# Attention tiles of two heads of both batches, a full-width g, and an h contracted over 64 rows with the batches side by side

## The chip, the cores and the metric

The kernel runs on one core of one Trainium2 chip. Times are device microseconds (us) of one launch on that core. The time before is the median of three runs, 1415.34 us (1413.17 to 1415.9). The profile comes from one more execution of its own, which took 1413.25 us; its span from the first to the last instruction is 1411.5 us.

## The reference, cut to what matters

Three layers follow each other. The first is a linear attention with 32 memory slots per head (8 batches, 8 heads, 576 positions, 64 columns a head), the second a maximum over three products, the third a gated one.

```python
a    = softmax(phi over the sequence)                 # 576 x 32 a head
k_m  = a.T @ k ;  v_m = a.T @ v                       # 32 x 64 a head
attn = softmax(q @ k_m.T / 8)                         # 576 x 32 a head
x    = attn @ v_m                                     # heads side by side: 4608 x 512
h    = max(x @ w1, x @ w2, x @ w3)                    # 4608 x 768
x2   = h @ w_out                                      # 4608 x 512
out  = (sigmoid(x2 @ w_gate) * (x2 @ w_val)) @ w_out2 # 4608 x 512
```

The kernel never forms x. For each batch it multiplies v_m by w1, w2 and w3 first, which gives g (256 rows for the 8 heads and their 32 slots), and then h = max over the three of g.T @ attn. The weights arrive as 64-bit floats and are turned into 32-bit ones on the chip. Products that need more than one pass split each operand into a high and a low part and add three passes (low by high, high by low, high by high).

## The kernel before, in words

**Phases.** The batches are taken in four pairs, p = 0 to 3. A pair has an *h stage* of 24 steps and an *x2 stage* of 16 steps; after the last pair comes the third layer (`up`, `down`), which the change does not touch. A prelude ahead of pair 0 loads and computes the first four attention tiles.

**Attention tiles.** Tile n = 4p .. 4p+3 is one batch and four of its heads, 128 partitions of 4 heads by 32 slots. Six stages make it: `a0` (exponential of phi), `a1` (transposes), `a2` (a.T @ [k v], four 32-column products side by side on TensorE, then a copy of each head's 32 rows into a zeroed block-diagonal tile), `a3` (transposes; `vt` is filled from two batches), `a4` (scores, two 64-column products side by side), `a5` (softmax), and `a_split` (high and low part, the tile `attn`). The tiles of pair p+1 are made between the steps of pair p.

**The h stage.** For every block j of 128 columns of h (6 blocks) there are four steps u, one for each batch and half of the sequence. `g_step` (line 342) makes 128 rows of g for block j+1 with three matmuls of 384 columns: 64 rows belong to one batch, 64 to the other, and they go to two different tiles, so that each of g's tiles holds 128 rows (4 heads) of one batch. They are copied out as two pieces of 64 partitions on ACT (line 356), and the low part is made by two subtractions on DVE (line 73; on POOL for 6 of the steps of pair 0). `h_step` (line 369) then runs 18 matmuls of 128 contracted rows by 288 columns into three PSUM banks, ACT copies one bank (line 379), DVE takes two maxima (lines 380, 381), ACT or DVE writes the high part (lines 68, 70) and POOL the low part.

**The x2 stage.** `x2_step` (line 392): 18 matmuls of 128 rows by 288 columns over all six blocks of h, one copy (three buffers), one store.

**Weights.** Each of 80 pieces of weights is loaded as 64-bit words into a ring of three buffers (`raw`), turned into floats by two ACT operations (lines 122, 123) and three DVE operations (lines 124, 125, 126, the last of which frees the buffer), and then split into high and low parts (w1 to w3, w_out) or stored again as floats (`wbf`, the 48 pieces of the third layer, `b_step`). In the program 24 pieces of w1 to w3 and 8 of w_out belong to the prelude and to pair 0; the 48 pieces of the third layer are asked for from pair 1 on. Pairs 1 to 3 load the split w1 to w3 back (`wxs`).

**What sets the order.** All transfers are issued from the SP queue, in order. On each engine the instructions stand in one fixed order, which a list scheduler chooses when the program is built, from its own model of how long each instruction takes: an instruction whose inputs are ready early in that model can be put ahead of instructions that the program writes before it. On the chip each engine then works through its list strictly in that order and waits where an input is not there. The eight PSUM banks are one pool (`bank()`).

Of the kernel before, what the change touches and what calls it, by code (L numbers as in the profile page):

```python
# [18 lines left out]
def attn_moe_kernel(  # L19
# [15 lines left out]
    J = wx.shape[0]  # L35
# [101 lines left out]
    def early(shape):  # L137

        t = low.tile([128, 2 * U], F32R, tag="h", name="early", bufs=4 * J)
        return f32(t[:, :shape[1]])  # L140

    def load_phi(n):
        st = A[n] = {"kv": [], "q": []}
        if n in (2, 3):
            st["phi"] = early([128, S])
        else:
            st["phi"] = att.tile([128, S], F32, tag="phi", name="phi", bufs=2)
        dma(st["phi"], phiT[n])

    def load_kv(n):  # L150
        for c in range(5):
            if n < 4:
                t = early([128, 512])
            else:
                t = att.tile([128, 512], F32, tag="kv", name="kv", bufs=7)
            if c < 4:
                dma(t, kvm[n, c])
            else:
                dma(t[:64], kvt[n])
            A[n]["kv"].append(t)  # L160

    def load_q(n, e):
        if (n, e) in ((0, 0), (0, 1)):
            t = early([128, S])
        else:
            t = att.tile([128, S], F32, tag="q", name="q", bufs=3)
        dma(t, qT[n, e])
# [3 lines left out]
    KVB = []  # L171
    for i in range(2):
        t = att.tile([128, 2, 2, 64], F32, name=f"kvb{i}")
        pool.memset(t, 0.0)
        KVB.append(t)

    def a0(n):
# [8 lines left out]
        vec.reciprocal(out=rs, in_=rs)  # L186
        yield
# [12 lines left out]
    def a2(n):  # L200
# [13 lines left out]
        kvb = st["kvb"] = KVB[n % 2]  # L214
        for s in range(4):
            r = slice(32 * s, 32 * s + 32)
            act.activation(out=kvb[r, :, s % 2], in_=p[r, :128].rearrange("p (x d) -> p x d", x=2),
                           func=AF.Copy, scale=st["rs"][r])
# [3 lines left out]
    def a3(n):  # L222
        st = A[n]
        b, g = divmod(n, 2)
# [6 lines left out]
        if b % 2 == 0:  # L231
            VT[b // 2, g] = mid.tile([128, 2, 4, 64], F32R, tag="vt", name="vt", bufs=4)
        vt = VT[b // 2, g]
        src = p[:, 128:256].rearrange("p (h m) -> p h m", h=2)
        for h in range(2):
            x = 3 * h if b % 2 == 0 else 2 - h
            act.copy(vt[:, 0, x], src[:, h])
            sub(vec, vt[:, 1, x], src[:, h], f32(vt[:, 0, x]))
# [95 lines left out]
    def g_step(p, j, hp):  # L334
        g, e = divmod(hp, 2)
        if e == 0:
            for b in range(2):
                G[b, j, g] = mid.tile([128, 2, 384], F32R, tag=f"g{b}", name=f"g{b}", bufs=3 + b)
# [530 lines left out]
```

## Time and profile before

| what | value |
| --- | --- |
| median of three runs | 1415.34 us |
| the profiled execution, its time / its span | 1413.25 / 1411.5 us |
| TensorE (PE) busy, share of the span | 1353.1 us, 96% |
| DVE / ACT / POOL busy | 875.0 / 583.3 / 517.7 us |
| prelude, until the first h matmul | 0 to 51 us |
| pair 0: h stage, x2 stage | 51 to 160, 160 to 212 us |
| pair 1: h stage, x2 stage | 212 to 298, 298 to 350 us |
| pair 2: h stage, x2 stage | 350 to 429, 429 to 473 us |
| pair 3: h stage, x2 stage | 473 to 540, 540 to 578 us |
| third layer | 578 to 1411 us |

The stage limits are the starts and ends of the matmuls of lines 369 and 392 in the trace. All four pairs do the same h and x2 work; pairs 0 to 2 also make attention tiles, and the weight pieces fall into the first two. A row of the stage view gives the time of the stage, then for each engine its busy time and its instructions, then the granted clock of TensorE, the busy share of the DMA engines and what they moved. A group row ends with busy time and mean time of one, and then the idle time ahead of the group and who ended it.

### The profile page before, as it was taken

Reading aid. Unit: us, or ns where it says so; the run is one execution under the profiler, and the core shown is the slowest. Engines: PE = TensorE matmul, PEld = TensorE weight load, DVE = VectorE, ACT = ScalarE, POOL = GpSimd, SP = SyncE. Lnnn points to the kernel's source line nnn. Section 1 sums busy time; section 2 is a strip of 40 time slices with the busy share of each in tenths; the row PEclk is TensorE's granted clock in tenths of the full one; section 3 lists DMA queues with packets and bytes.
Section 4 is the critical chain, followed back from the end, with each engine's and each line's share of the span. In section 5 each row is a group of like instructions: output and inputs, shape, how many; then the busy total and the mean of one; then the engine's idle time right before and its main releaser. Section 6 shows DMA issues by size and latency. Waiting matters only on the chain.

```text
span 1411.5 us, 22167 instructions
## 1 busy us (share of the span) xinstructions
PE 1353.1 (96%) x7864; PEld 1191.1 (84%) x7864; DVE 875.0 (62%) x1532; ACT 583.3 (41%) x1236; POOL 517.7 (37%) x456
## 2 busy tenths in 40 slices
PE   6588899989999999999999999999999999999998
PEld 3478798879999999878888888888888899999997
DVE  5989989987773575667765344454454534554454
ACT  6768667754653353353333221232222322133221
POOL 2666422241233126554487111371112712161211
PEclk8779999999999999999999999999999999999999
DMA  9588799878552433775546554465454666566651
GB/s 316 192 260 278 257 328 321 291 249 276 185 162 92 159 95 119 281 265 213 204 175 228 167 179 161 160 198 194 149 168 175 209 219 229 188 230 225 223 202 67
DMA packets 112269, 292.43 MB, mean 207 GB/s; under 512 B 12576, under 2 KB 28960, under 8 KB 112160
## 3 DMA queue, kind: packets, MB, share of 16 engines
q1 hardware_dynamic: 112160, 291.03, 60.8%
q8 instruction: 62, 1.02, 0.3%
q14 instruction: 47, 0.39, 0.1%
HBM read 224.92 MB, written 66.06 MB: 206 GB/s over the span
## 4 chain that ended last, share of the span: by engine, by line
PE 80%; DVE 7%; DMA 5%; issue 3%; ACT 3%; POOL 1%; SPq 0%; DVEq 0%; POOLq 0%; ACTq 0%
PE po L754 21%; PE px L687 15%; PE ps L369 11%; PE pz L687 10%; PE pv L687 10%; PE ps L392 8%; PE ps L342 3%; DMA raw<-wb_dram 1%; DVE ca L124 1%; DVE g L73 1%; PE ps L245 1%; DVE ca L126 1%; ACT g L356 1%; PE ps L207 1%; DMA q<-qT_dram 1%
## 5 line engine op out<-in xcount | busy, mean ns | idle before, releaser
L754 PE MATMUL po<-wo,gg 128*128 128x512 f32 x1296 | 332.8, 395 | 1.0 <-POOL gg L73 1.0
L73 POOL TENSOR_TENSOR gg<-gf,gg 128x512 fp32r<-128x512 f32 (+1 forms) x120 | 143.5, 1196 | 478.1 <-ACT gg L720 478.1
L754 PEld LDWEIGHTS po<-wo,gg 128*128 128x128 f32 x1296 | 242.5, 188 | 55.2 <-POOL gg L73 1.5
L369 PE MATMUL ps<-attn,g 128*128 128x288 f32 x1728 | 258.3, 304 | 18.3 <-POOL s L73 5.6
L369 PEld LDWEIGHTS ps<-attn,g 128*128 128x128 f32 x1728 | 247.5, 195 | 26.1 <-POOL s L73 5.9
L687 PE MATMUL px<-xa,tb 128*128 128x512 f32 (+1 forms) x1080 | 245.3, 369 | 1.6 <-ACT sg L710 1.3
L766 DVE TENSOR_TENSOR acc<-po,acc 128x512 f32<-128x512 f32 x180 | 124.3, 691 | 182.7 <-PE po L754 182.2
L687 PEld LDWEIGHTS px<-xa,tb 128*128 128x128 f32 x1080 | 198.1, 188 | 31.6 <-POOL tb L73 1.7
L687 PE MATMUL pz<-xa,tb 128*128 128x512 f32 (+1 forms) x720 | 171.0, 370 | 0.4 <-DVE x L70 0.4
L687 PE MATMUL pv<-xa,tb 128*128 128x512 f32 (+1 forms) x720 | 170.6, 369 | 0.0
L392 PE MATMUL ps<-h,wo 128*128 128x288 f32 x1152 | 161.4, 299 | 0.0
L392 PEld LDWEIGHTS ps<-h,wo 128*128 128x128 f32 x1152 | 157.3, 192 | 2.2 <-issue 1.9
L73 POOL TENSOR_TENSOR h<-hm,h 128x288 fp32r<-128x288 f32 x96 | 82.9, 865 | 196.7 <-ACT h L68 102.8
L687 PEld LDWEIGHTS pz<-xa,tb 128*128 128x128 f32 x720 | 132.2, 188 | 20.7 <-DVE x L70 0.8
L687 PEld LDWEIGHTS pv<-xa,tb 128*128 128x128 f32 x720 | 131.8, 188 | 18.9
L720 ACT CAST gg<-gf 128x512 fp32r<-128x512 f32 (+1 forms) x120 | 69.4, 579 | 179.6 <-DVE gf L716 132.7
L738 DVE TENSOR_TENSOR u<-pz,p 128x512 f32<-128x512 f32 (+1 forms) x120 | 76.2, 635 | 95.3 <-PE pz L687 89.2
L73 DVE TENSOR_TENSOR g<-ps,g 64x384 fp32r<-64x384 f32 x180 | 99.3, 552 | 32.7 <-ACT g L356 29.3
L356 ACT CAST g<-ps 64x384 fp32r<-64x384 f32 x192 | 90.7, 474 | 56.4 <-PE ps L342 30.4
L710 ACT ACTIVATE sg<-sg 128x512 f32<-128x512 f32 (+1 forms) x90 | 53.1, 590 | 146.8 <-DVE sg L708 146.6
L73 POOL TENSOR_TENSOR xa<-xf,xa 128x512 fp32r<-128x512 f32 (+1 forms) x64 | 78.7, 1252 | 19.9 <-ACT xa L131 19.9
L342 PE MATMUL ps<-wx,vt 128*128 128x384 f32 x288 | 73.0, 365 | 7.3 <-DVE g L73 3.0
(91 smaller groups left out, 1415.6 us busy)
## 6 DMA issues: line engine op xcount, KB each, us to landing
tb<-tbs SPq DMA_DIRECT2D x168, 512.0 KB, 3.7
wx<-wxs SPq DMA_DIRECT2D x72, 384.0 KB, 4.1
wo<-wos SPq DMA_DIRECT2D x48, 512.0 KB, 5.1
tbs<-tb SPq DMA_DIRECT2D x42, 512.0 KB, 2.9
raw<-wb_dram SPq DMA_DIRECT2D x48, 384.0 KB, 4.8
kv<-kvm_dram SPq DMA_DIRECT2D x48, 256.0 KB, 5.2
raw<-wx_dram SPq DMA_DIRECT2D x24, 384.0 KB, 4.0
wxs<-wx SPq DMA_DIRECT2D x24, 384.0 KB, 5.0
```

What stands on the lines that cost most here:

```text
L73: eng.tensor_tensor(out=o, in0=a, in1=b, op=ALU.subtract)
L124: vec.tensor_scalar(out=ai, in0=ai, scalar1=3, scalar2=None, op0=ALU.logical_shift_left)
L342: pe.matmul(ps[:, :384], lhsT=vt[:, x, 2 * e:2 * e + 2].rearrange("p a m -> p (a m)"), rhs=w[:, y], start=(n == 0), stop=(n == 2),)
L356: act.copy(t[r, 0], ps[r, :384])
L369: pe.matmul(ps[w][:, :U], lhsT=G[b, j, g][:, x, 128 * w:128 * w + 128], rhs=at[:, y, hf * U:hf * U + U], start=(n == 0), stop=(n == 5),)
L392: pe.matmul(ps[:, :U], lhsT=wo1_t[:, x, (d * J + j) * 128:(d * J + j) * 128 + 128], rhs=H[u, j][:, y], start=(n == 0), stop=(n == 3 * J - 1),)
L687: pe.matmul(ps[:, :half], lhsT=w[:, a, o:o + 128], rhs=x[:, k, c, :half], start=(first and n == 0), stop=(n == 5), skip_group_check=not first,
L710: act.activation(out=sg, in_=src, func=AF.Sigmoid)
L720: act.copy(t[:, 0, :half], gf)
L738: vec.tensor_tensor(out=u, in0=ps[:, :half], in1=E["p1", v], op=ALU.add)
L754: pe.matmul(ps, lhsT=GG[sc, j, c, h][:, x, 128 * m:128 * m + 128], rhs=WO[sc, j, h][:, y], start=(n == 0), stop=(n == 5),)
L766: vec.tensor_tensor(out=t, in0=ps, in1=t, op=ALU.add)
```

## The change

An attention tile now holds two heads of *both* batches of the pair (partitions 0 to 63 one batch, 64 to 127 the other), so phi, k, v and q are loaded in two pieces for a tile (k and v in runs of 256 columns rather than 512). In `a2` two copies of 128 partitions with a masked scale (`rm`, one more small DVE operation in `a0`) replace four copies of 32 partitions. `vt` is one tile for one attention tile, copied whole. `g_step` copies 128 partitions once on ACT and subtracts once on DVE, never on POOL.

`h_step` becomes `h_part`. A block j has two parts, one for each half of the sequence, and a part computes both batches: for each of three weights, four tiles and three passes there are two matmuls of 64 contracted rows by 288 columns, one on partitions 0 to 63 and one on 64 to 127, into two banks. There are 72 of them in a part, in two half steps of 36, so a part holds up to six of the eight banks. Afterwards ACT copies two banks, DVE takes four maxima, ACT writes the high part over 576 columns at once (DVE writes none), and POOL the low part over 576 columns. `x2_step` reads the same values from the new tile; its output has two buffers instead of three. The eight pieces of w_out are asked for at other steps of pair 0.

```diff
 def a2: ...
-            act.activation(out=kvb[r, :, s % 2], in_=p[r, :128].rearrange("p (x d) -> p x d", x=2),
-                           func=AF.Copy, scale=st["rs"][r])
+        for e in range(2):
+            act.activation(out=kvb[:, :, e], in_=p[:, :128].rearrange("p (x d) -> p x d", x=2),
+                           func=AF.Copy, scale=st["rm"][:, e:e + 1])
 def g_step(p, j, hp):
 ...
-        src, eng = ps, vec
-        if p == 0 and hp == 0:
-            src, eng = mid.tile([128, 384], F32, tag="gf", name="gf", bufs=1), pool
-            act.copy(src, ps[:, :384])
-        for hf in range(2):
-            r = slice(64 * hf, 64 * hf + 64)
-            t = G[(hf + e) % 2, j, g]
-            act.copy(t[r, 0], ps[r, :384])
-            sub(eng, t[r, 1], src[r, :384], f32(t[r, 0]))
+        t = G[j, hp] = mid.tile([128, 2, 384], F32R, tag="g", name="g", bufs=8)
+        act.copy(t[:, 0], ps[:, :384])
+        sub(vec, t[:, 1], ps[:, :384], f32(t[:, 0]))
...
-    def h_step(p, j, u):
+    def h_part(p, j, hf, first):
+        if first:
+            HP[j, hf] = []
+        for w, hp in [(w, hp) for w in range(3) for hp in range(4)][slice(0, 6) if first else slice(6, 12)]:
+            if hp == 0:
+                HP[j, hf].append([bank() for _ in range(2)])
+            at = AT[4 * p + hp]
+            for n, (x, y) in enumerate(PASSES):
+                for b in range(2):
+                    r = slice(64 * b, 64 * b + 64)
+                    pe.matmul(
+                        HP[j, hf][w][b][:, :U],
+                        lhsT=G[j, hp][r, x, 128 * w:128 * w + 128],
+                        rhs=at[r, y, hf * U:hf * U + U],
+                        start=(hp == 0 and n == 0), stop=(hp == 3 and n == 2),
+                    )
+        yield
+        if first:
+            return
+        ps = HP.pop((j, hf))
+        m = mid.tile([128, 2, U], F32, tag="hm", name="hm", bufs=2)
+        for b in range(2):
+            act.copy(m[:, b], ps[0][b][:, :U])
+        for w in (1, 2):
+            for b in range(2):
+                vec.tensor_tensor(out=m[:, b], in0=ps[w][b][:, :U], in1=m[:, b], op=ALU.max)
+        t = low.tile([128, 4 * U], F32R, tag="h", name="h", bufs=2 * J)
+        t = t.rearrange("p (two b t) -> p two b t", two=2, b=2)
+        H[hf, j] = t
+        act.copy(t[:, 0], m)
+        sub(pool, t[:, 1], m, f32(t[:, 0]))
...
-                at(22 + n / 2, w_step)
+                at((22, 22, 24, 25, 27, 28, 30, 30)[n], w_step)
...
-                gens.append(h_step(p, j, u))
+                gens.append(h_part(p, j, u // 2, u % 2 == 0))
```

The scheduler chooses the orders anew, and the diff does not show what it makes of them. Three places follow, each before and then in the changed program; the tile that an instruction writes stands left of the arrow, and the line numbers are those of each program.

DVE, before, near the end of pair 0's h stage (lines 380 and 381 are the maxima of h, line 70 its high part, lines 124 to 126 a conversion of a weight piece, `sm` belongs to the softmax):

```order
L381 TENSOR_TENSOR hm<-ps,hm 128x288 x2
L124 TENSOR_SCALAR ca<-ca 128x384
L180 TENSOR_REDUCE nm<-phi 128x1
L70 CAST h<-hm 128x288
L125 ISA ca<-ca,cr 128x768
L270 TENSOR_REDUCE sm<-s 128x18
L126 SCALAR_TENSOR_TENSOR ca<-raw,ca 128x384
L380 TENSOR_TENSOR hm<-ps,hf 128x288
```

The same place in the changed program (line 397 is a maximum):

```order
L397 TENSOR_TENSOR hm<-ps,hm 128x288 x2
L126 SCALAR_TENSOR_TENSOR ca<-raw,ca 128x384
L288 TENSOR_REDUCE sm<-s 128x18
L124 TENSOR_SCALAR ca<-ca 128x384
L289 TENSOR_SCALAR sm<-sm 128x18
L125 ISA ca<-ca,cr 128x768
L290 RECIPROCAL sm<-sm 128x18
L126 SCALAR_TENSOR_TENSOR ca<-raw,ca 128x384
L124 TENSOR_SCALAR ca<-ca 128x384
L125 ISA ca<-ca,cr 128x768
L293 STREAM_TRANSPOSE stg<-s 128x576
L126 SCALAR_TENSOR_TENSOR ca<-raw,ca 128x384
```

Conversions of the third layer's weights have moved in between the maxima of pair 0. Counted through the whole list: before, 33 of the 80 conversions stand ahead of the last maximum of pair 0 and 67 ahead of the last one of pair 1; in the changed program 26 stand ahead of the 24th of the 48 maxima of pair 0, 45 ahead of the 32nd, 65 ahead of the 40th, and all 80 ahead of the last.

SP, before, at the start of pair 0's x2 stage (`raw` loads a weight piece, `wbf` stores a converted one, `x2s` is the result of an x2 step):

```order
L53 DMA raw<-wb_dram 128x384
L53 DMA x2s<-x_2104 128x288
L53 DMA q<-qT_dram 128x576 x2
L53 DMA wbf<-ca 128x384
L53 DMA x2s<-x_2139 128x288
```

The same place in the changed program:

```order
L53 DMA raw<-wb_dram 128x384
L53 DMA wbf<-ca 128x384
L53 DMA raw<-wb_dram 128x384
L53 DMA wbf<-ca 128x384 x3
L53 DMA phi<-phiT_dram 64x576 x2
L53 DMA x2s<-x_2265 128x288
```

All loads and stores of the weight pieces now stand ahead of the first store of x2. Up to the 80th load the SP list of the changed program moves 68 MB, from the 33rd to the 80th load 33 MB; before it was 55 MB between those two.

TensorE, before, inside an h stage (line 342 is `g_step`, line 369 `h_step`):

```order
L342 MATMUL ps<-wx,vt 128x384 x3
L369 MATMUL ps<-attn,g_861 128x288 x9
L342 MATMUL ps<-wx,vt 128x384 x3
L369 MATMUL ps<-attn,g_861 128x288 x9
L369 MATMUL ps<-attn,g_979 128x288 x18
```

In the changed program (line 357 is `g_step`, line 382 `h_part`, lines 218 and 219 transposes of an attention tile):

```order
L357 MATMUL ps<-wx,vt 128x384 x3
L382 MATMUL ps<-attn,g 128x288 x36
L218 MATMUL ps<-ident,et 128x128 x4
L219 MATMUL ps<-ident,et 64x128
L357 MATMUL ps<-wx,vt 128x384 x3
L382 MATMUL ps<-attn,g 128x288 x36
```

Where 18 matmuls over 128 rows stood between two `g_step`s, 36 over 64 rows stand now, in two row halves that alternate. In the lists of pairs 1 to 3 the array goes 60 times from a 128-row matmul of another kind to the 64-row ones and 50 times back where it stayed in one form before; three more pairs of changes come from `a2` being split between x2 steps.

More of the change, by code (lines that the diff above doesn't have):

```diff
@@ L135, in attn_moe_kernel, with early_tile, early, source @@
     A = {}
-    def early(shape):
-        t = low.tile([128, 2 * U], F32R, tag="h", name="early", bufs=4 * J)
-        return f32(t[:, :shape[1]])
+    halves = []
+    def early_tile():
+        return f32(low.tile([128, 4 * U], F32R, tag="h", name="early", bufs=2 * J))
+    def early(cols):
+        if not halves:
+            t = early_tile()
+            halves.extend((t[:, :2 * U], t[:, 2 * U:]))
+        return halves.pop(0)[:, :cols]
+    def source(n, b):
+        p, hp = divmod(n, 4)
+        g, pr = divmod(hp, 2)
+        return 2 * (2 * p + b) + g, pr ^ b
     def load_phi(n):
@@ L186, in a0 @@
         vec.reciprocal(out=rs, in_=rs)
+        rm = st["rm"] = att.tile([128, 2], F32, tag="rm", name="rm", bufs=4)
+        vec.tensor_scalar(out=rm, in0=mask, scalar1=rs, scalar2=None, op0=ALU.mult)
         yield
@@ L230, in a3 @@
         act.copy(kt, p[:, 0:128])
[L231 to L238, printed above, removed]
+        vt = VT[n] = mid.tile([128, 2, 128], F32R, tag="vt", name="vt", bufs=8)
+        act.copy(vt[:, 0], p[:, 128:256])
+        sub(vec, vt[:, 1], p[:, 128:256], f32(vt[:, 0]))
     def a4(n):
@@ L334, in g_step @@
     def g_step(p, j, hp):
[L335 to L338, printed above, removed]
         ps = bank()
-        vt, w = VT[p, g], WX.pop((j, hp))
+        vt, w = VT[4 * p + hp], WX.pop((j, hp))
         for n, (x, y) in enumerate(PASSES):
@@ new lines, in g_step @@
+        act.copy(t[:, 0], ps[:, :384])
+        sub(vec, t[:, 1], ps[:, :384], f32(t[:, 0]))
+    H = {}
+    HP = {}
+    def h_part(p, j, hf, first):
[6 more added lines that the diff above has]
+            for n, (x, y) in enumerate(PASSES):
+                for b in range(2):
+                    r = slice(64 * b, 64 * b + 64)
@@ L374, in h_step @@
                     )
-                    n += 1
         yield
-        h = mid.tile([128, U], F32, tag="hf", name="hf", bufs=2)
-        m = mid.tile([128, U], F32, tag="hm", name="hm", bufs=2)
-        act.copy(h, ps[0][:, :U])
-        vec.tensor_tensor(out=m, in0=ps[1][:, :U], in1=h, op=ALU.max)
-        vec.tensor_tensor(out=m, in0=ps[2][:, :U], in1=m, op=ALU.max)
-        t = low.tile([128, 2 * U], F32R, tag="h", name="h", bufs=4 * J).rearrange("p (two t) -> p two t", two=2)
-        H[u, j] = t
@@ L384, in h_step @@
-        copy(vec if u == 0 else act, t[:, 0], m)
+        if first:
+            return
+        ps = HP.pop((j, hf))
+        m = mid.tile([128, 2, U], F32, tag="hm", name="hm", bufs=2)
+        for b in range(2):
+            act.copy(m[:, b], ps[0][b][:, :U])
+        for w in (1, 2):
+            for b in range(2):
+                vec.tensor_tensor(out=m[:, b], in0=ps[w][b][:, :U], in1=m[:, b], op=ALU.max)
+        t = low.tile([128, 4 * U], F32R, tag="h", name="h", bufs=2 * J)
+        t = t.rearrange("p (two b t) -> p two b t", two=2, b=2)
@@ L399, in x2_step @@
         yield
-        t = low.tile([128, U], F32, tag="x2", name="x2", bufs=3)
+        t = low.tile([128, U], F32, tag="x2", name="x2", bufs=2)
         copy(vec if u % 2 == 0 or p == NP - 1 else act, t, ps[:, :U])
```

61 lines of the change are left out of this document (27 added, 34 removed).

## The prediction

> **What bounds the kernel now.** I read the stage view first: time, then busy time and instructions of PE, PEld, DVE, ACT and POOL, then the granted clock, the DMA share and GB/s.
>
> ```profile
> 0.00:51.00 51.00, 29.50 (x236) 15.98 (x236) 35.01 (x73) 33.16 (x81) 22.28 (x27) 0.83 0.86 283
> 51.00:160.00 109.00, 91.54 (x604) 83.15 (x605) 101.17 (x191) 80.30 (x188) 67.20 (x62) 0.86 0.75 250
> 160.00:212.00 52.00, 49.52 (x410) 46.14 (x408) 46.21 (x98) 31.76 (x74) 15.07 (x13) 0.97 0.90 307
> 212.00:298.00 86.00, 81.92 (x659) 76.05 (x658) 82.92 (x182) 63.16 (x154) 26.71 (x27) 0.98 0.88 304
> 298.00:350.00 52.00, 45.88 (x358) 44.22 (x356) 39.87 (x80) 24.91 (x58) 11.91 (x10) 0.93 0.79 261
> 350.00:429.00 79.00, 79.00 (x662) 74.93 (x662) 56.78 (x126) 47.57 (x116) 27.13 (x30) 1.00 0.51 160
> 429.00:473.00 44.00, 44.00 (x356) 42.64 (x354) 13.33 (x28) 11.86 (x29) 8.20 (x8) 1.00 0.40 135
> 473.00:540.00 67.00, 67.00 (x489) 67.00 (x488) 45.11 (x93) 34.59 (x82) 18.58 (x23) 1.00 0.31 94
> 578.00:1411.00 833.00, 826.76 (x3821) 702.99 (x3819) 428.51 (x638) 243.29 (x438) 288.74 (x239) 1.00 0.57 195
> ```
>
> The rows from 350 us on are TensorE's: its busy time is the whole stage, at full clock. The earlier h stages do the same matmuls in 109 and 86 us instead of 79, and there DVE is the full engine: 101.2 of 109 and 82.9 of 86 us. The second view is line 126, the last operation of a weight conversion, over the same stages:
>
> ```profile
> 0.00:51.00 51.00, 5.49 (x7) 0.83 0.86 283
> 51.00:160.00 109.00, 18.39 (x25) 0.86 0.75 250
> 160.00:212.00 52.00, 11.70 (x15) 0.97 0.90 307
> 212.00:298.00 86.00, 12.93 (x18) 0.98 0.88 304
> 298.00:350.00 52.00, 11.40 (x15) 0.93 0.79 261
> ```
>
> So 32 of the 80 conversions are done when pair 0's h stage ends at 160 us, and 48 are spread over the next three stages. The third view is the groups of the stage from 298 us:
>
> ```profile
> L126 DVE SCALAR_TENSOR_TENSOR ca<-raw,ca 128x384 uint32<-128x384 uint32 x15 | 11.4, 760 | 0.3
> L125 DVE CUSTOM_DVE_ANT_0 ca<-ca,cr 128x768 uint16<-128x768 uint16 x14 | 8.7, 618 | 1.0
> L122 ACT ACTIVATE ca<-raw 128x384 f32<-128x384 f32 x13 | 7.2, 550 | 12.4 <-DMA raw<-wb_dram 12.4
> L124 DVE TENSOR_SCALAR ca<-ca 128x384 uint32<-128x384 uint32 x14 | 6.7, 479 | 2.8 <-ACT ca L122 2.8
> ```
>
> A conversion costs DVE 0.48 + 0.62 + 0.76 = 1.86 us there. ACT waits 12.4 us for the loads, so where DVE has room the three load buffers are the next limit.
>
> **What the change takes away.** g is evicted at full width:
>
> ```profile
> L73 DVE TENSOR_TENSOR g<-ps,g 64x384 fp32r<-64x384 f32 x180 | 99.3, 552 | 32.7 <-ACT g L356 29.3
> L70 DVE CAST h<-hm 128x288 fp32r<-128x288 f32 x24 | 9.4, 392 | 0.3
> ```
>
> 180 subtractions become 96. Their time goes by columns, not by partitions (384 both times), so DVE saves 84 x 0.552 = 46 us, and 9 us of casts that ACT takes over. ACT saves about as much on g. But from 350 us on neither engine sets the pace, so there this is worth nothing; in pair 0, where 12 of 48 subtractions were POOL's, it is 12 x 0.552 + 6 x 0.392 = 9 us. The masked copies and `vt` save a few us of ACT beside that, the `rm` operations cost DVE some 2 us; both are inside the rounding.
>
> **What the new order adds.** The DVE list of the changed program has all 80 conversions ahead of the last maximum of pair 0's h stage. DVE works in order: behind each conversion stand maxima that free the banks and low parts of g that the matmuls need, and TensorE, in order too, has no other pair's h matmuls to go on with. So that stage cannot end before DVE has done 136.2 us (35.0 + 101.2 so far) + 48 x 1.86 = 89 us - 9 us = 216 us of work; with the 24 us that DVE was idle before 160 us, that is 240 us. The other limit is the ring of loads:
>
> ```profile
> 311.00:342.00 31.00, 28.50 (x197) 27.71 (x198) 23.69 (x49) 17.15 (x40) 3.88 (x3) 0.90 0.93 311
> 311.00:342.00 31.00, 6.05 (x9) 0.90 0.93 311
> DMA to landing us min/median/max: 2.8/4.5/7.3
> ```
>
> The rows are 311 to 342 us, all work and then line 126, and the landing of the weight loads. Nine conversions in 31 us are 3.4 us each with DVE a quarter idle, at 311 GB/s, that is 1.07 MB for each. In the new order only 33 MB / 47 = 0.70 MB go with each, 2.25 us at the same rate. The 26th conversion comes after 98 us of DVE work by the list (rows times durations), at about 115 us; 54 more at 2.25 to 3.4 us end at 237 to 299 us, at 2.8 us at 266. I take 255 us, between DVE's 240 and that: **+95 us** against 160 (bounds 225 and 290: +65 and +130).
>
> **What comes back.** The three stages from 160 to 350 us have no conversions left and should run as TensorE's do: 48 us for the x2 stage of pair 0 (the 44 of pair 2 and one more attention tile, some 4 us), 79 and 44 for pair 1, together 171 for 190: **-19 us** (bounds 0 and -19).
>
> **The 64-row matmuls.** Here the timeline of TensorE inside pair 2 carries the price of changing the array's form:
>
> ```profile
> 409.27 0.96 PE L369 MATMUL ps<-attn,g 128*128 128x288 f32 x6
> 410.16 1.43 PE L207 MATMUL ps<-kv,es 128*32 128x128 f32 x40
> ...
> 415.29 2.56 PE L369 MATMUL ps<-attn,g 128*128 128x288 f32 x18
> 417.77 0.95 PE L245 MATMUL ps<-q,kt 128*64 128x288 f32 x6
> ...
> 417.77 1.19 PE L245 MATMUL ps<-q,kt 128*64 128x288 f32 x8
> 418.90 1.32 PE L369 MATMUL ps<-attn,g 128*128 128x288 f32 x8
> ```
>
> 18 and 6 matmuls give (2.56 - 0.96) / 12 = 0.133 us each. The 32-column form starts 0.89 us after six of them, 0.095 more than 6 x 0.133; the 64-column form 2.48 us after 18, again 0.09 more. Coming back, eight take 1.32 us where 0.96 + 2 x 0.133 = 1.23 were due, 0.09 more, and the four 64-column pairs last 1.13 us up to there where they need 4 x 0.24 (the same run cut after three pairs is 0.95, after four 1.19): 0.17 more, for the first load and the way out. These pairs are two passes, so one pass of 288 columns is 0.12. That is some 0.38 us for there and back; 0.2 us a change with loads of 128 columns. That the rows alone change (128 to 64) costs the same is not in these rows; the bound below is nothing. The Trainium skill, TensorEngine Tiling (Array Packing), Key Properties, says that any change of tiling mode drains the array, which speaks for the upper value here; the trace agrees where the columns change, with its 0.09 us. From pair 1 on there are 60 + 50 + 6 = 116 changes on TensorE's path: **+23 us** (0 to 30). Those of pair 0 hide behind DVE.
>
> The pace of a pair is the other open price. Forty 32-column matmuls start within 1.36 us, 0.034 each, less than the 0.059 that 128 columns need at 0.133/288 a column, so column tiles do run side by side, and no slower than one. For two row halves I take the same, 0.133 us a pair: **0** for 3 x 432 pairs. Bounds: 0.12 (that one pass), -17 us; 0.266, one after the other, +172 us.
>
> **Covered edits.** The runs of 1 KB in the loads of k and v lie beside DVE's work in pair 0. Two x2 buffers instead of three:
>
> ```profile
> x2s<-x SPq DMA_DIRECT2D x64, 144.0 KB, 3.5
> ```
>
> a store lands in 3.5 us and two steps last 4.7 (two of 18 x 0.133), so the copy still finds a free buffer; without that cover it is about 0.3 us a step, 5 us in the last pair. A part holds six banks for two steps of 2.4 us; DVE's four maxima and two subtractions (2.9 us of each 5.8) keep up once the conversions are gone.
>
> **The sum.** 95 - 19 + 23 + 0 = +99 us. Against the profiled execution's own 1413.25 us that is 1512; the median of the runs shown lies 2.1 us above it, so **1514 us**.
>
> **The rivals.**
> *B, the row halves do not run fully side by side.* Nothing in the trace shows row halves; for them speak the column tiles. If the weights of the two halves load one after the other, a pair takes two loads. A load of 128 columns is about 0.105 us, twice the 0.05 that the 64-column form lost at its first load, so 0.21 for a pair: 1296 x 0.077 = +100, 1614 us. Entirely in a row it is 1514 + 172 = 1686. (The Trainium skill, TensorE: Matmul & The Clock Gate, Part 3, gives 3.07 times for four row tiles, 77% of ideal; by it a pair would be 0.173 us, an estimate of +52 us and 1566. No run here shows it.) Pair 0 does not care: 432 x 0.21 still ends before 255.
>
> *C, the hoisted conversions come cheaper.* POOL is on for 67.2 of 109 us in pair 0 and for 11.9 of 52 later; with it off the three operations have these least times:
>
> ```profile
> L124 DVE TENSOR_SCALAR ca<-ca x80: 307/354/1921, 19.0 to 344.9; 128x384 uint32<-128x384 uint32 x80
> L125 DVE CUSTOM_DVE_ANT_0 ca<-ca,cr x80: 483/558/1784, 19.5 to 345.7; 128x768 uint16<-128x768 uint16 x80
> L126 DVE SCALAR_TENSOR_TENSOR ca<-raw,ca x80: 500/557/1740, 20.1 to 346.3; 128x384 uint32<-128x384 uint32 x80
> ```
>
> At the medians, 1.47 us, the 48 cost 71 us instead of 89, and the first 32 shrink by some 20: the stage ends at about 200 if the loads keep up. +40 - 19 + 23 = +44, 1459 us. Against it: the loads would have to come every 1.9 us or so.
>
> *D, not slower.* The same place, priced to the end: it decides from 156 us on (160 + 19 - 23), so DVE would have to finish pair 0's h stage earlier than now with 48 more conversions in it. Ending at 150 it would give 1409 us. Even at the least times (1.29 us each) the 48 alone are 62 us, so I leave it a trace of chance.
>
> **How the numbers follow.** The forecast (order decides, pairs side by side) has 0.74, its own range 1480 to 1550; B 0.18, C 0.05, D 0.03. The range 1465 to 1605 holds the forecast's cases, half of C and the milder half of B. 0.2% (2.8 us) is about what can be told from no change here: slower 0.96 (all but D and a little), same 0.01, faster 0.03.
>
> **What would show it.** Right: the first x2 matmul comes at about 255 us instead of 160, with 80 of line 126 before it; the next four stages show TensorE without idle time; 64-row matmuls start in twos with about 0.133 us from pair to pair, and the first after a `g_step` comes 0.1 us late. Wrong: DVE idle for long in pair 0 (then loads or TensorE set the pace), or h stages of 110 to 145 us in pairs 2 and 3 (B).

## The result, and the profile after

The changed kernel takes 1556.99 us (median of four runs, 1553.73 to 1558.23), the kernel before beside it 1415.53 us: a ratio of 1.100, 95% interval 1.0978 to 1.1021. The span of the profiled execution is 1556.5 us.

The stage view of the changed kernel (time, then busy time and instructions of PE, PEld, DVE, ACT and POOL, granted clock, DMA share, GB/s). The stages are pair 0's h stage in two pieces, its x2 stage, the h and x2 stages of pairs 1 and 2 (pair 2's x2 stage left out), pair 3's h stage, and the third layer:

```profile
46.00:146.00 100.00, 69.78 (x552) 56.86 (x552) 60.94 (x118) 44.45 (x96) 34.33 (x29) 0.71 0.56 186
146.00:294.00 148.00, 73.22 (x488) 58.84 (x489) 106.21 (x216) 71.05 (x154) 24.00 (x19) 0.59 0.80 253
294.00:348.00 54.00, 51.71 (x407) 48.35 (x407) 21.22 (x46) 14.59 (x34) 12.06 (x9) 0.89 0.51 157
348.00:435.00 87.00, 85.54 (x1093) 73.90 (x1092) 44.71 (x106) 33.74 (x82) 22.64 (x18) 1.00 0.53 165
435.00:480.00 45.00, 45.00 (x356) 42.84 (x354) 11.83 (x27) 9.93 (x24) 9.31 (x7) 1.00 0.43 132
480.00:565.00 85.00, 85.00 (x1090) 73.57 (x1089) 42.17 (x100) 33.50 (x80) 22.41 (x17) 1.00 0.49 149
...
610.00:685.00 75.00, 75.00 (x923) 67.02 (x923) 29.88 (x67) 24.53 (x56) 15.66 (x11) 1.00 0.25 77
...
723.00:1556.00 833.00, 817.97 (x3818) 703.18 (x3816) 426.54 (x639) 244.07 (x441) 292.94 (x241) 1.00 0.57 197
```

The third layer lasts 833 us as before. All that was lost lies ahead of it, and nearly all of that in pair 0: the first x2 matmul comes at 293.6 us instead of 160.0. There no engine is full: of 248 us TensorE works 143, DVE 167. The conversions are where the prediction had them. Line 126, the last operation of a conversion, over the same two pieces (busy time and count, then clock, DMA share, GB/s):

```profile
46.00:146.00 100.00, 14.68 (x21) 0.71 0.56 186
146.00:294.00 148.00, 33.09 (x53) 0.59 0.80 253
```

And the waits of the second piece (who waited <- for whom: us, times, longest), the largest of ACT, DVE and TensorE among them:

```profile
POOL h L73 <- ACT h L401: 81.3, 5, 28.1
ACT ca L122 <- DMA raw<-wb_dram: 39.9, 27, 7.1
DVE ca L124 <- ACT ca L122: 27.8, 28, 6.6
...
PE ps L382 <- ACT hm L394: 16.4, 4, 6.0
PE ps L250 <- ACT kvb L241: 16.3, 2, 11.2
```

ACT waits for loads 27 times, DVE then 28 times for ACT, and TensorE waits behind ACT, for banks that it has to empty and for its copy of an attention tile (line 241). The 26th conversion ends at 145.8 us and the 80th at 297.9: 2.82 us each, 54 times. That is a mean of two paces: the six up to the 32nd conversion, the last ones of w_out, end at 170.3 us, 4.1 us each, and the 48 of the third layer take 2.66 us each.

From pair 1 on the changed kernel is TensorE's, with hardly anything else in the way. One piece of its timeline in pair 3 (start, duration, engine, line and tile, count; line 357 is `g_step`, line 382 `h_part`):

```profile
609.37 0.68 PE L357 MATMUL ps<-wx,vt 128*128 128x384 f32 x3
609.98 2.64 PE L382 MATMUL ps<-attn,g 64*128 64x288 f32 x36
612.55 0.79 PE L357 MATMUL ps<-wx,vt 128*128 128x384 f32 x3
613.27 2.65 PE L382 MATMUL ps<-attn,g 64*128 64x288 f32 x36
```

36 matmuls of 64 rows take 2.64 us to their modelled end, where 18 of 128 rows took 2.56 us before. From the start of one half step to the next it is 3.3 us (609.98 to 613.27), where it was 2.9: two changes of the array's form lie in between. The same place in the kernel before:

```profile
473.06 2.54 PE L369 MATMUL ps<-attn,g 128*128 128x288 f32 x18
475.44 0.69 PE L342 MATMUL ps<-wx,vt 128*128 128x384 f32 x3
475.97 2.57 PE L369 MATMUL ps<-attn,g 128*128 128x288 f32 x18
```

Set side by side, stage by stage (from the first matmul of a stage to the first of the next), after minus before: pair 0 up to its x2 stage +133.6, its x2 stage +2.6; pair 1 h +0.6, x2 -6.9; pair 2 h +6.4, x2 +0.6; pair 3 h +7.5, x2 +0.2. Sum +144.6 us.

### The profile page after: what moved, and what is told of

It is laid out like the page before. It is cut to its first block, busy times and chain, and to the rows that moved or that the text cites. A ratio compares the mean times of both kernels' runs of the same rounds, so it can differ in the third digit from the quotient of the medians.

```text
span 1556.5 us, 25132 instructions
## 1 busy us (share of the span) xinstructions
PE 1413.3 (91%) x9592; PEld 1221.4 (78%) x9592; DVE 803.4 (52%) x1425; ACT 522.1 (34%) x1062; POOL 487.8 (31%) x394
## 4 chain that ended last, share of the span: by engine, by line
PE 75%; DMA 6%; DVE 3%; issue 3%; ACT 2%; POOL 1%; SPq 0%; DVEq 0%; ACTq 0%; POOLq 0%
PE po L772 19%; PE px L705 14%; PE ps L382 11%; PE pz L705 9%; PE pv L705 9%; PE ps L410 8%; DMA raw<-wb_dram 4%; PE ps L357 3%; DMA x2s<-x 1%; DMA phi<-phiT_dram 1%; PE ps L232 1%; ACT ca L122 1%; DVE ca L126 1%; PE ps L263 1%; DVE ca L124 1%
## 5 line engine op out<-in xcount | busy, mean ns | idle before, releaser
L382 PE MATMUL ps<-attn,g 64*128 64x288 f32 x3456 | 297.6, 324 | 63.4 <-ACT hm L394 23.3
L382 PEld LDWEIGHTS ps<-attn,g 64*128 64x128 f32 x3456 | 268.1, 207 | 96.4 <-ACT hm L394 26.4
L772 PE MATMUL po<-wo,gg 128*128 128x512 f32 x1296 | 327.1, 392 | 1.0 <-POOL gg L73 1.0
L73 POOL TENSOR_TENSOR h<-hm,h 128x576 fp32r<-128x576 f32 x48 | 68.9, 1436 | 322.2 <-ACT h L401 322.2
L705 PE MATMUL pv<-xa,tb 128*128 128x512 f32 (+1 forms) x720 | 169.8, 367 | 0.0
L73 DVE TENSOR_TENSOR g<-ps,g 128x384 fp32r<-128x384 f32 x96 | 53.1, 553 | 85.8 <-ACT g L365 85.6
L397 DVE TENSOR_TENSOR hm<-ps,hm 128x288 f32<-128x288 f32 x192 | 78.2, 448 | 23.6 <-PE ps L382 23.4
L357 PE MATMUL ps<-wx,vt 128*128 128x384 f32 x288 | 81.1, 393 | 3.1 <-ACT wx L131 2.9
```

The costliest lines, as they stand in the source:

```text
L73: eng.tensor_tensor(out=o, in0=a, in1=b, op=ALU.subtract)
L357: pe.matmul(ps[:, :384], lhsT=vt[:, x], rhs=w[:, y], start=(n == 0), stop=(n == 2),)
L382: pe.matmul(HP[j, hf][w][b][:, :U], lhsT=G[j, hp][r, x, 128 * w:128 * w + 128], rhs=at[r, y, hf * U:hf * U + U], start=(hp == 0 and n == 0 ...
L397: vec.tensor_tensor(out=m[:, b], in0=ps[w][b][:, :U], in1=m[:, b], op=ALU.max)
L705: pe.matmul(ps[:, :half], lhsT=w[:, a, o:o + 128], rhs=x[:, k, c, :half], start=(first and n == 0), stop=(n == 5), skip_group_check=not first,
L772: pe.matmul(ps, lhsT=GG[sc, j, c, h][:, x, 128 * m:128 * m + 128], rhs=WO[sc, j, h][:, y], start=(n == 0), stop=(n == 5),)
```

## The experiments

For all runs, the numbers that the text below uses: the first x2 matmul of pair 0, the h stages of pairs 1, 2 and 3 (first h matmul to first x2 matmul, from the trace), and the time. A run without an interval was timed once. The time of the kernel before is that of the medians taken beside these runs. The stages are those of the profiled execution, which took 6 us more than the median in e1_pin and 4 more in e3_group.

| kernel | x2 of pair 0 starts | h of pair 1 | pair 2 | pair 3 | time, us | ratio to before, 95% interval |
| --- | --- | --- | --- | --- | --- | --- |
| before | 160.0 | 86.1 | 78.7 | 67.3 | 1412.6 to 1415.6 | |
| changed | 293.6 | 86.7 | 85.1 | 74.8 | 1557.0 | 1.0978 to 1.1021 |
| e1_pin | 208.2 | 100.4 | 95.1 | 103.4 | 1527.1 | 1.0782 to 1.0837 |
| e2_ring4 | 273.4 | 86.0 | 85.1 | 74.8 | 1537.6 | 1.0858 to 1.0902 |
| e5_other_lists | 205.7 | 123.2 | 85.2 | 74.8 | 1524.4 | 1.0747 to 1.0796 |
| e6_before_other | 165.4 | 90.6 | 87.0 | 67.7 | 1445.7 | 1.0205 to 1.0241 |
| e3_group | 191.6 | 94.0 | 93.8 | 106.1 | 1507.4 | 1.0643 to 1.0691 |
| e9_phi | 177.2 | 95.3 | 94.8 | 105.1 | 1496.7 | 1.0561 to 1.0604 |
| e8_spread | 177.8 | 90.6 | 90.2 | 70.4 | 1440.3 | 1.0153 to 1.0193 |
| e12_tiles_free | 176.5 | 88.7 | 83.8 | 70.4 | 1438.1 | 1.0151 to 1.0184 |
| e13_four | 177.1 | 97.8 | 82.2 | 67.4 | 1447.5 | 1.0214 to 1.0245 |
| e4_apart | 209.0 | 100.6 | 93.5 | 108.0 | 1533.8 | |
| e10_eighteen | 233.6 | 127.7 | 127.7 | 111.9 | 1606.0 | |
| e11_same_rows | 242.8 | 140.2 | 140.2 | 127.7 | 1659.3 | |

### Are the hoisted conversions the cause? (e1_pin)

```diff
-        vec.tensor_scalar(out=ai, in0=ai, scalar1=3, ...)          # line 124
+        ins = vec.tensor_scalar(out=ai, in0=ai, scalar1=3, ...)
+        if pin:                                # pin is True for the third layer's pieces only
+            tc.keep_in_program_order(ins)
```

> The changed kernel with one thing added: the first DVE operation of each conversion of a third-layer weight piece (48 of the 80) must stay on DVE's list behind the instruction that the program writes just before it. 32 conversions then stand ahead of the last maximum of pair 0 instead of 80, 40 at the end of pair 1's h stage, 53 at pair 2's, 80 at pair 3's. Mine (the new order of the conversions is what cost pair 0 its time): pair 0's first x2 matmul comes at 150 to 165 us instead of 293.6, the stage from 46 us lasts 100 to 118 us instead of 247; the 48 conversions spread over later stages of which some are DVE's, some 10 us back; the 7 us per pair of form changes stay; 1425 to 1445 us in all. Rival (pair 0 is slow because its 64-row halves, its full-width g or its attention tiles are, whatever DVE's list): the first x2 matmul stays behind 250 us, and the time above 1500.

Nearly two thirds of pair 0's loss. The first x2 matmul comes 85 us earlier, but 48 us later than before the change, and the time falls by 30 us only. The stage view, pair 0's h stage, then those of pairs 1 and 3:

```profile
46.00:207.00 161.00, 115.24 (x1035) 95.24 (x1035) 95.48 (x192) 70.78 (x158) 55.76 (x47) 0.73 0.57 182
...
256.00:356.00 100.00, 90.04 (x1092) 76.37 (x1091) 57.39 (x127) 37.76 (x93) 22.73 (x17) 0.98 0.59 185
...
557.00:660.00 103.00, 87.80 (x918) 75.59 (x919) 67.70 (x133) 42.13 (x96) 17.97 (x11) 0.92 0.54 177
```

Two things that my expectation did not hold show here. Pair 0 is slow without any of the 48 conversions in it, with DVE at work for 95 of 161 us; the 26th conversion ends at 145.4 us, as late as in the changed kernel. And the conversions, put back where the program writes them, cost pairs 1 to 3 some 68 us that the changed kernel did not lose there, although DVE is far from full. The timeline of pair 3 shows how (the last number of a row is the idle time ahead of it and its releaser):

```profile
593.20 0.55 ACT L122 ACTIVATE ca<-raw 128x384 f32<-128x384 f32 x1 [4.39 <-DMA raw<-wb_dram]
...
596.32 0.55 ACT L122 ACTIVATE ca<-raw 128x384 f32<-128x384 f32 x1 [2.14 <-DMA raw<-wb_dram]
596.77 0.46 ACT L367 CAST g<-ps 128x384 fp32r<-128x384 f32 x1
...
597.27 0.56 DVE L73 TENSOR_TENSOR g<-ps,g 128x384 fp32r<-128x384 f32 x1 [4.87 <-ACT g L367]
...
597.88 0.79 PE L359 MATMUL ps<-wx,vt 128*128 128x384 f32 x3 [2.40 <-DVE g L73]
```

ACT stands in front of two loads of weight pieces; the copy of g is behind them on its list, DVE waits for the copy, TensorE for DVE. DVE's list was mended, ACT's was not.

### The ring of load buffers (e2_ring4)

```diff
-        raw = pl.tile([128, PC], I64, tag="raw", name="raw", bufs=3)
+        raw = pl.tile([128, PC], I64, tag="raw", name="raw", bufs=4)
...
-        vt = VT[n] = mid.tile([128, 2, 128], F32R, tag="vt", name="vt", bufs=8)
+        vt = VT[n] = mid.tile([128, 2, 128], F32R, tag="vt", name="vt", bufs=6)
...
-        mx = att.tile([128, S // 32], F32, tag="mx", name="mx", bufs=2)
+        mx = att.tile([128, S // 32], F32, tag="mx", name="mx", bufs=1)
```

> The changed kernel with four load buffers for the weight pieces instead of three (paid for with six vt tiles instead of eight and one mx tile instead of two); the DVE list still has all 80 conversions in pair 0. Mine (from the 26th conversion on pair 0 goes at the pace of the ring of loads, 2.7 to 2.8 us a conversion, DVE idle for a third of it): a conversion comes every 2.1 us, so the 54 end 35 us earlier, pair 0's h stage ends at about 245 us, 1515 to 1530 us in all. Rival 1 (DVE's own work sets it): no more than 5 us. Rival 2 (the transfers share one rate, so more buffers only make each slower): under 10 us, loads landing later than the 3.9 us of now.

19 us less than the changed kernel, between my expectation and the second rival's. From the 25th to the 80th conversion it takes 2.57 us each (137.5 to 278.8 us) instead of 2.83 (142.0 to 297.9): 15 of the 19 us. The loads of third-layer pieces, changed kernel:

```profile
raw<-wb_dram SPq DMA_DIRECT2D x48, 384.0 KB, 3.9
```

and with four buffers:

```profile
raw<-wb_dram SPq DMA_DIRECT2D x48, 384.0 KB, 4.4
```

So both of the readings hold in part: the ring is a limit, and with a fourth load on the way each lands half a microsecond later. DVE's own work isn't the limit in either (106 us busy of 148 in the changed kernel's second piece, 99.8 of 129 here from 138 us on).

### Other lists for both kernels (e5_other_lists, e6_before_other)

The scheduler has a second mode, which doesn't use its model of durations. One edit, in the changed kernel and in the one before:

```diff
-    with _tile.TileContext(nc, schedule_with_timeline_sim=True) as tc:
+    with _tile.TileContext(nc, schedule_with_timeline_sim=False) as tc:
```

> The changed kernel, its lists made by the scheduler's other mode, which does not use the model of how long each instruction takes. 46 conversions then stand ahead of the last maximum of pair 0 (80 in the changed kernel, 32 when pinned), 80 by the eighth maximum of pair 1's second half. The same instructions in another order. Mine (the order of the lists, not the work, makes pair 0 slow): pair 0's h stage ends between 185 and 235 us, its first four blocks take clearly less than the 131 to 138 us that they take in the changed and in the pinned kernel, and pair 1 carries 34 conversions; 1455 to 1520 us. Rival (the new work makes pair 0 slow, whatever the order: parts of 72 matmuls that hold six banks, POOL's and ACT's pieces of 576 columns): the first four blocks still take 120 us or more.

> The kernel before, its lists made by the same other mode (32 conversions ahead of pair 0's last maximum, 58 at pair 1's, 80 in pair 2). This is the yardstick for the run of the changed kernel in that mode. If that mode is as good as the usual one, within 1% of 1413 us; then the difference between these two runs is the change without the hoist that the usual mode made: mine +50 to +100 us (23 for the changes of form, the rest pair 0's slow first half and the 14 conversions more). Rival (the change itself costs next to nothing, all of it is the order): under +30.

Pair 0's h stage ends at 201 us, and its first four blocks take 93 us (59.2 to 151.9) instead of 131 to 138, with the same new work in them. They begin 13 us later, but about a third of their time went with the lists, and the rival's 120 us are out. What is left of them is still longer than the 70 us of the same blocks in e6_before_other, and the 77 in the kernel before in the usual mode: some 20 us there go with the change in either comparison. The 34 conversions of pair 1 make its h stage 37 us longer, so the whole gains just 33 us, and its 1524.4 us lie 4 above my range. That mode is itself 2.2% worse for the kernel before, not within 1%. In this mode the change costs 1524.4 - 1445.7 = 79 us, where it costs 142 in the usual one: 63 us go with the lists that one mode happened to make. Since the lists of the two kernels differ in both modes, 79 us is no pure price of the work either.

### What else is slow in pair 0 (e3_group, e9_phi)

On top of e1_pin, the two `g_step`s of a part stand ahead of its two half steps:

```diff
-                if j + 1 < J:
+                if j + 1 < J and u % 2 == 0:
                     gens.append(g_step(p, j + 1, u))
+                    gens.append(g_step(p, j + 1, u + 1))
```

> The pinned kernel (as e1_pin) with the two g_steps of a part ahead of its two half steps, so that TensorE goes 63 times into the 64-row form instead of 85 times, of which some 17 fewer in pairs 1 to 3. Mine (a change of form costs 0.16 to 0.19 us each way): 17 x 2 x 0.18 = 6 us less than e1_pin in pairs 1 to 3, up to 8 with pair 0, if the banks keep up. Rival (the extra 7 us per pair are not the changes but waits for banks at the part's ends): no gain, or a loss, as two g banks more are wanted at once.

20 us instead of 6 to 8, and 17 of them in pair 0, where I had expected 2. The h stages of pairs 1 to 3, slowed by ACT as above, changed by -6.4, -1.3 and +2.7 us, which says nothing on the changes of form. Why pair 0 gains is not told apart: the grouping also gives every engine a new list.

Then one pin more, on DVE's maximum over phi (`nm`), the first operation of an attention tile. In the changed kernel DVE's timeline in pair 0 shows what it is about:

```profile
112.64 0.55 DVE L126 SCALAR_TENSOR_TENSOR ca<-raw,ca 128x384 uint32<-128x384 uint32 x1
118.85 0.75 DVE L203 TENSOR_REDUCE nm<-phi 128x1 f32<-128x576 f32 x1 [5.67 <-DMA phi<-phiT_dram]
119.52 0.81 DVE L397 TENSOR_TENSOR hm<-ps,hm 128x288 f32<-128x288 f32 x2
```

DVE stands 5.7 us in front of a load of phi that SP issued at 113.6 us, with two maxima of h behind it, for which TensorE waits 4.9 us.

```diff
-        vec.tensor_reduce(out=nm, in_=st["phi"], axis=AX.X, op=ALU.max, negate=True)
+        tc.keep_in_program_order(vec.tensor_reduce(out=nm, in_=st["phi"], ...))
```

> The grouped kernel (as e3_group) with one pin more: the maximum over phi that begins an attention tile stays on DVE's list behind the instruction that the program writes before it, instead of being put ahead of maxima of h. In e3_group DVE stands 12.5 us in four of these before pair 0's h stage ends, waiting for phi to land. Mine (DVE's place in line for phi is one of the things that make pair 0's first half slow): DVE's wait for phi falls under 4 us there, the stage ends 6 to 12 us earlier than 191, 1495 to 1502 us. Rival (the other waits take its place): under 3 us.

In e3_group DVE's waits in pair 0's h stage had this row:

```profile
DVE nm L205 <- DMA phi<-phiT_dram: 12.5, 4, 5.8
```

In e9_phi the group is gone, the first x2 matmul comes 14.4 us earlier, and the time is 1496.7 us, 10.7 less. This place in line was one of the causes. 17 us of pair 0's loss (177.2 against 160.0) are left; no run of mine separates them.

### All repairs together (e8_spread)

Beside e9_phi: ACT's first operation of a third-layer conversion is pinned as DVE's is, and

```diff
-        while len(bq) < 2 and bplan:
+        while len(bq) < 3 and bplan:
...
-            n_b = 22 if last else 13
+            n_b = 12 if last else 18
```

> All repairs together: grouped g_steps, the pins of e9_phi, ACT's first operation of a third-layer conversion pinned as well, three loads on the way instead of two, and 18, 18 and 12 conversions in pairs 1, 2 and 3 instead of 13, 13 and 22. In e1_pin ACT stood 46 us of 90 in pair 3 in front of a load of a weight piece, with the copy of g for TensorE behind it. Mine (in pair 3 the waits come from ACT's list, not from DVE's work): pair 3's h stage falls from 103 to 71 to 78 us, pairs 1 and 2 from 98 and 93 to 82 to 88, pair 0's ends at 180 to 185; 1435 to 1460 us. Rival (conversions cost their 2 us each wherever they lie): 1480 or more. Neither expects it below the kernel before.

The time is as expected: 1440.3 us, 56 less than e9_phi. The h stages of pairs 0 to 3:

```profile
45.00:177.00 132.00, 104.75 (x1029) 89.65 (x1030) 95.12 (x192) 70.73 (x160) 59.32 (x50) 0.82 0.67 217
...
226.00:316.00 90.00, 83.45 (x1086) 73.77 (x1086) 62.52 (x135) 42.81 (x102) 22.77 (x17) 0.99 0.73 229
...
363.00:453.00 90.00, 83.72 (x1088) 73.88 (x1086) 62.33 (x133) 42.78 (x101) 22.73 (x17) 1.00 0.68 219
...
500.00:571.00 71.00, 71.00 (x923) 66.87 (x921) 54.40 (x101) 33.33 (x78) 15.73 (x11) 1.00 0.52 170
```

Pair 3 now carries 12 conversions and TensorE never stops. The 48 conversions cost 85 us in the changed kernel's pair 0 and 68 in e1_pin's later pairs; spread out, asked for early and pinned on both engines they cost little. From the start of pair 1 to the end of pair 3's h stage it takes 345 us, against 404 in e1_pin and 336 in the changed kernel, which has no conversion there; most of the waiting that is left in pairs 1 and 2 is 4.0 us in front of a transpose ahead of each x2 stage. That the changed kernel would be 117 us faster by nothing but order, one more load on the way and the places of the conversions is shown by this run; each part's share isn't, since ACT's pin, the third load and the spread came together. No run gives the kernel before the same repairs, so the 25 us or so that it stays ahead by are no price of the change alone.

### The pin on phi, and all g_steps of a block together (e12_tiles_free, e13_four)

```diff
+        if n < 8:                                                  # e12: pin phi's maximum in pair 0 only
             tc.keep_in_program_order(ins)
...
+                k = 4 if p else 2                                  # e13: all four g_steps of a block together
+                if j + 1 < J and u % k == 0:
+                    gens.extend(g_step(p, j + 1, u + i) for i in range(k))
```

> The kernel of e8_spread with the pin on the maximum over phi only for the tiles made ahead of or during pair 0. In e8_spread TensorE stands 5 us at the start of the x2 stages of pairs 1 and 2 (311.4 to 316.7 and 449.0 to 453.9 us) in front of a transpose of an attention tile whose maximum DVE's list, by the pin, has behind a conversion. Mine: these two gaps go, 8 to 10 us less, 1430 to 1434 us. Rival (without the pin DVE stands before phi in these pairs, as the changed kernel does, 37.6 us in all, and TensorE feels it): no gain, h stages of pairs 1 and 2 longer than 85 us.

> The kernel of e12_tiles_free with all four g_steps of a block together in pairs 1 to 3 (two and two in e12): two changes of form fewer for each of 15 blocks. Mine (0.16 to 0.19 us a change, whatever stands between): 15 x 2 x 0.18 = 5 us less than e12, pair 3's h stage 68 to 69 us. Rival (four banks for g and four for the first half of a part are all eight, so TensorE waits for the eviction of the part before): no gain or up to 15 us more.

e12: the two gaps are gone (the last h matmul ends at 313.0 and 446.2 us, the first x2 matmul starts at 313.5 and 446.6), and the h stages of pairs 1 and 2 are 8.3 us shorter, but their x2 stages are 5.6 us longer; 1438.1 against 1440.3 us is not the 8 to 10 that I gave. e13: pair 3 does what the changes of form promise, down to 67.4 us, and pair 1 takes it back with waits of one kind:

```profile
PE ps L256 <- ACT kvb L247: 9.7, 3, 4.6
```

TensorE stands in front of an attention tile's transposes (0.9 us in e12). This is not quite the rival's wait for banks, and the price is in its range. Neither beats the kernel before.

### How the row halves run (e4_apart, e10_eighteen, e11_same_rows)

In the changed kernel the two matmuls of a pair are neighbours on TensorE's list. On top of e1_pin they are put three and three apart, on top of e8_spread 18 and 18, and in e11, again on top of e8_spread, both are on the same rows:

```diff
-            for n, (x, y) in enumerate(PASSES):
-                for b in range(2):
+            for b in range(2):                                     # e4
+                for n, (x, y) in enumerate(PASSES):
...
+        for b, (w, hp) in [(b, a) for b in range(2) for a in part]:   # e10; part: the six (w, hp) of a half step
...
-                    r = slice(64 * b, 64 * b + 64)
+                    r = slice(0, 64)                               # e11
```

> The pinned kernel (as e1_pin) with the loop over the row halves outside the loop over the passes: three matmuls on rows 0 to 63, then three on rows 64 to 127, instead of taking turns. Same count, same work. Mine (a pair costs 0.131 us because neighbours in the queue lie on different rows): neighbours overlap only where the half changes, so six matmuls take between 4 x 0.131 (one overlap at each change) and 6 x 0.131 instead of 3 x 0.131; 1296 pairs of pairs 1 to 3 cost 57 to 170 us more, pair 3's h stage 94 to 130 us instead of 75. Rival (TensorE looks ahead in its queue by row halves, or the rate is that of the operands): pair 3's h stage stays at 75 us.

> The kernel of e8_spread with the row halves 18 apart: of each half step the 18 matmuls on rows 0 to 63 first, then the 18 on rows 64 to 127. In e4_apart they stood three and three on the list, and yet their starts came in twos, 5 to 12 ns apart, at 0.131 us from two to two. Mine now (TensorE starts a matmul of the other row half past matmuls that wait for theirs, but not past any number of them): pair 3's h stage, 70.2 us in e8_spread, goes to between 85 and 127 us (127 is 70 + 432 x 0.131, no overlap at all). Rival 1 (it looks ahead 18 and more): it stays within 2 us of 70. Rival 2 (a 64-row matmul takes 0.066 us by itself, no overlap of halves needed): it stays at 70 too; e11_same tells it from rival 1.

> The kernel of e8_spread with both matmuls of a pair on rows 0 to 63: the second batch's products are left out and the first's are made twice, count and sizes as before. Mine (a 64-row matmul of 288 columns takes 0.131 us as a 128-row one does, and only the other row half runs beside it): 0.131 us from start to start, pair 3's h stage 120 to 130 us instead of 70. Rival (a matmul of half the rows takes half the time, 0.066 us): it stays at 70.

Timelines from pair 3, 72 matmuls (a part) without anything between them. e8_spread:

```profile
500.53 5.01 PE L386 MATMUL ps<-attn,g 64*128 64x288 f32 x72
```

e10_eighteen:

```profile
636.17 8.61 PE L387 MATMUL ps<-attn,g 64*128 64x288 f32 x72
```

e11_same_rows:

```profile
661.77 9.74 PE L386 MATMUL ps<-attn,g 64*128 64x288 f32 x72
```

And 36 of e4_apart:

```profile
577.14 2.65 PE L384 MATMUL ps<-attn,g 64*128 64x288 f32 x36
```

On the same rows a matmul takes 0.133 us, so the halves do run side by side, and fully: 72 in 5.01 us. Three and three apart costs nothing (2.65 us for 36, as in the changed kernel). My expectation for that run is refuted: the program's list for TensorE holds them three and three all through pairs 1 to 3, so TensorE does start matmuls past others that stand ahead of them. Eighteen and eighteen apart it keeps a quarter of the overlap: 9.74 - 8.61 = 1.13 us, or 8.6 matmuls at 0.131, at the three places of a part where the row half changes, about three each. e4_apart's long h stage in pair 3 (108.0) is e1_pin's trouble with ACT (103.4), not the halves'.

## Why the prediction was right, and where it was not

**Direction and place: right, the size not.** The forecast was 1514 us with slower at 0.96; it is 1557, slower and 43 us off. That is inside 1465 to 1605, but outside the 1480 to 1550 that I gave the forecast's own case: the wide range, opened for half of C and the milder half of B, covers a miss that has nothing to do with either. The loss sits in pair 0's h stage, with 78 of the 80 conversions done before the first x2 matmul, and from pair 1 on the stages run at TensorE's pace.

**The new order in pair 0: right in kind, mis-sized, +134 instead of +95.** It is the term that failed, beyond its own bounds (+65 and +130). I gave two limits, DVE's work (240 us) and the ring of loads (266), and took 255. DVE was no limit: it is busy for 167 of the 248 us. The 54 conversions come every 2.82 us, close to the 2.8 that I took from 3.4 and 2.25, but partly by luck: it is the mean of 4.1 us for six of w_out, which take as long in e1_pin (145.4 to 169.8 us), and 2.66 us for the 48; e2_ring4 shows that the ring is a limit. What was wrong is where its 54 conversions begin. I had the 26th at about 115 us, from 98 us of DVE work with 17 us of idle time; it came at 145.8, after 88 us of work and 58 of idle time. Those 31 us are most of the 39 that the term is short of; the rest is that I took 255, 11 us short of the 266 of my own ring limit. Behind the 115 us stood a silent assumption, that DVE stays as full in the first half of the stage as it was before. It did not: the new lists made it wait for phi and for ACT (10 and 26 us from 46 to 146 us), and e1_pin shows the first half as slow with no hoisted conversion at all. With the `g_step`s grouped the 26th conversion ends at 137.9 us (e3_group), with the pin on phi's maximum at 125.3 (e9_phi). By the first x2 matmul, and in this order of repairs, the runs divide the 134 us into 85 for the hoisted conversions (e1_pin), 17 that the grouping of `g_step`s mends in some way (e3_group), 14 for DVE's place in front of phi (e9_phi), and 17 that stay open. TensorE's own busy time in the stage also rose, from 91.5 to 143 us, at a granted clock of 0.71 and 0.59 against 0.86; how much of the 134 us comes by that slower clock and how much by the waits is not separated.

**What comes back: -19 forecast, about -11 measured.** Pair 1's stages came as forecast (86.7 us, which is 79 and 7.7 for the changes of form, and 45.1). Pair 0's x2 stage took 54.8 us instead of 48: its first two steps take 4.7 and 4.1 us where the third takes 2.6, at a granted clock of 0.89 over the stage, and TensorE waits 2.3 us for a copy of an attention tile.

**The changes of form: right, 0.19 us.** In pair 3 a block takes 11.65 us from start to start before (473.06 to 484.71), 13.2 in the changed kernel with eight changes (609.98 to 623.2), 12.42 in e8_spread with four, 12.02 in e13_four with two:

```profile
507.52 9.80 PE L388 MATMUL ps<-attn,g 64*128 64x288 f32 x144
517.25 2.36 PE L363 MATMUL ps<-wx,vt 128*128 128x384 f32 x12
519.54 1.72 PE L388 MATMUL ps<-attn,g 64*128 64x288 f32 x22
```

So a change costs (13.2 - 11.65) / 8 = 0.19, 0.77 / 4 = 0.19, 0.37 / 2 = 0.19. The upper value, which the rows of before alone did not prove for a change of rows, was the one to take. My working was looser than its result: the parts that I read off the rows, 0.09, 0.17 and 0.09, add up to 0.35 us for there and back, not 0.38. Pairs 1 to 3 paid 7.7 (over the 79 above), 6.4 and 7.5, 21.6 us for the 23 forecast.

**The pace of a pair: right, 0.131 us.** Rival B falls by the trace (the 0.05 us at a first load, from which it priced a load, stands in no row: they give 0.17 for load and way out together), and e11_same_rows shows what it would have cost had the halves not overlapped (127.7 us for pair 3's h stage instead of 70.4). The estimate of 0.173 us from the factor for four row tiles (the Trainium skill, TensorE: Matmul & The Clock Gate, Part 3) isn't borne out for two; that its 1566 us come nearest to the measured time is chance.

**Rival C** had a point that didn't help it. The conversions did come cheaper (33.09 / 53 = 0.62 us for line 126 against 0.76), but the loads took the place of the work, as the prediction's last sentence on C said. **D** falls with the first x2 matmul at 293.6 us. The sign that I named for being wrong, DVE idle for long in pair 0, was seen, and it pointed to the right term.

**Expectations that failed:** e1_pin by 82 us, because I took a conversion's cost to be DVE's alone, where a late load on ACT's list did the harm; e4_apart, because I took TensorE's list to be strict; e12_tiles_free by 4 to 8 us, since its x2 stages gave back most of the gain; e13_four, which lost 9 us where I had 5 to gain; e2_ring4 by 8 us and e5_other_lists by 4; and e3_group, which gained 20 us for 6 to 8.

## What to carry to other kernels

When a change moves instructions on in-order engines, the new list has to be read on every engine, not only on the one that was full: here 117 of 142 us came back without touching the new arithmetic, by keeping a few first instructions (those that wait for a transfer) behind the work that others wait for, and by asking for their data one step earlier. A limit worked out as "work plus the idle time of before" holds only while the engine stays as full as before, so bound the idle time too. And a packed matmul form pays for every change into and out of it, so its neighbours of the other form belong together, as long as banks and evictions can take them.

## What the runs showed of the hardware

Two row halves of 64 rows run at the pace of one (0.131 us for a pair of them, 0.133 for each matmul on the same rows), and a change between 128 and 64 rows costs 0.19 us, as a mean of the way in and the way out.

I had not expected TensorE to take matmuls out of the order of its list, and wrote ahead of the prediction that every engine keeps strictly to it. For the row halves that does not hold: with three of one half ahead of three of the other it loses nothing, with 18 ahead of 18 it still overlaps about three per change of half. The Trainium skill, TensorE: Matmul & The Clock Gate, Part 3, The mechanism, says that matmuls start in strict order and only weight loads are pulled ahead; the 2.65 us for 36 in e4_apart don't agree, since in strict order six matmuls would take four steps of 0.131 us instead of three, a third more; the measurement decides.

The granted clock is low where TensorE stalls: 0.59 in the changed kernel's second piece of pair 0 (TensorE busy for half of it), 0.73 and 0.82 in e1_pin's and e8_spread's pair 0, 1.00 where TensorE is hardly ever idle. At the lower clock the same matmuls take longer: 36 of them take 4.08 us at 0.61 (587.45 us of e4_apart) and 2.65 us at 1.00. A stalled stage so loses a second time; no run here separates that part.
